# Loads in 1-KB runs, tokens kept by residue of four, and a list scheduler's engine orders, in a windowed attention followed by a gated MLP

## Chip, cores and metric

One core of one Trainium2 chip. The metric is device time in microseconds (us); a lower one is better. Every timed comparison below has runs of the kernel before on the same chip in the same rounds. The changed kernel was not run again beside the experiments, so where one is set against it, medians of different rounds and chips are compared; the kernel before had medians of 329.6 to 333.0 us in all of them. A run counts as slow when it is over 1.5% above the fastest of its kernel; ratios use fast runs alone. The output must match the reference; four experiments break that, and say so.

## The reference, cut

Eight batches, eight heads, 576 tokens, 64 columns per head. Heads 0 to 3 look back over 32 tokens ("plain"), heads 4 to 7 over 32 tokens at a distance of four ("dilated"). The result x (576 x 512 per batch) goes through a gated MLP with a shift by one token.

```python
mask_plain = (rel >= 0) & (rel < 32)
mask_dil   = (rel >= 0) & (rel < 128) & (rel % 4 == 0)      # heads 4..7
attn = softmax(where(mask, q @ k.T / 8, -1e9)) @ v          # [8, 8, 576, 64], f32
x  = attn.transpose(0, 2, 1, 3).reshape(8, 576, 512)
xk = mu_k * x + (1 - mu_k) * x_prev                         # "mixing", x_prev: x one token earlier
xr = mu_r * x + (1 - mu_r) * x_prev
k  = relu(xk @ w_k)                                         # 512 -> 1024
out = sigmoid(xr @ w_r) * (k * k @ w_v)                     # 1024 -> 512
```

## The kernel before

Tiles of q, k, v are loaded per batch; TensorE makes scores, ScalarE exponentials, VectorE masks and normalizes; the result is transposed into `xT` (columns on partitions). `interp` mixes neighbouring tokens, and the MLP runs on tiles of 512 tokens. Attention of batch p and MLP of tile p-1 are woven by hand-given costs. The parts that matter here:

```python
p_s = tc.tile_pool(name="p_s", bufs=1, space=PSUM)   # scores, 2 banks
p_o = tc.tile_pool(name="p_o", bufs=2, space=PSUM)   # attention outputs and transposes
p_k = tc.tile_pool(name="p_k", bufs=2, space=PSUM)   # x @ w_k
p_v = tc.tile_pool(name="p_v", bufs=2, space=PSUM)   # x @ w_r, k2 @ w_v

def load(b):
    for nm, src, lst in (("q", q, qn), ("k", k, kn)):           # plain heads: runs of 256 B, SP
        for h in range(4):
            nc.sync.dma_start(out=t[:, h], in_=src[b, h].rearrange("(c p) d -> p c d", p=96))
    # ... dilated q and k: "h (p r) d -> p h (r d)", runs of 1 KB, cast on the way (GpSimd queue)
    # ... plain v in six windows of 128 tokens, runs of 256 B (SP)
    for r in range(4):                                          # dilated v: runs of 256 B, cast on the way
        nc.gpsimd.dma_start(out=VD1[i][:, r, :, 0:64], in_=vr[0:112, r, 4:8])
    # ... casts of q (DVE), k and v (POOL)

def interp(t0, n):
    dx = wrk.tile([128, 4, n], FP16, name=f"dx{n}", bufs=1)
    nc.gpsimd.tensor_tensor(out=dx, in0=xo, in1=xT[:, :, 1 + t0:1 + t0 + n], op=ALU.subtract)
    for mu, dst in ((nmk, xk), (nmr, xr)):
        # per column chunk: tm = dx * mu (DVE); then dst = tm + xT (DVE)
        ...
```

The softmax here doesn't subtract the row's maximum and nothing guards it: scores larger than these inputs give would overflow.

## Time and profile before

| | kernel before |
|---|---|
| median of four runs (lowest, highest) | 331.25 us (328.71, 413.53) |
| profiled span | 332.9 us |
| first MLP matmul (pk, the product with w_k) | 48.0 us |
| mixing of batch 1 done | 104.6 us |
| six periods, batch 1's mixing to batch 7's | 186.0 us, 31.0 each |
| from the last batch's mixing to the end | 42.3 us |

"Mixing done" is the end of the addition that makes `xk` for the last tokens of a batch. The three lower rows make up the span: 104.6 + 186.0 + 42.3 = 332.9. "Period n" is the stretch that ends with batch n's mixing. The kernel before mixes each batch in two parts, 384 tokens and 192: by the first parts the account is 93.1 + 190.1 + 49.7. The lines that the start rests on (start, length, engine, line, what, count, idle time before):

```profile
48.03 3.70 PE L381 MATMUL pk<-xk,wk 128*128 128x384 f16 x12
...
67.81 2.72 PE L381 MATMUL pk<-xk,wk 128*128 128x384 f16 x8 [14.62 <-DMA VD<-in_v_dram]
```

and of VectorE, the second part of batch 1, on which the first pk that reads batch 1 (at 104.7 us) waits:

```profile
104.07 0.56 DVE L338 TENSOR_TENSOR xk<-tm,xT 128x768 f16<-128x768 f16 x1
```

So the MLP begins at 48.0 us, and 67.8, which the prediction takes for its first matmul, is where it goes on after a hole of 14.6 us. The queues of the profile's page (packets, MB, share of the 16 DMA engines' time):

```profile
q1 hardware_dynamic: 86496, 29.31, 41.4%
q0 software_dynamic: 35920, 10.23, 31.9%
```

In these kernels the transfers that SP issues are on the hardware queue, those that GpSimd issues, the only ones that cast on the way, on the software queue. 41.4% of 332.9 us is 138 us of full activity, 31.9% is 106: 244 us in all. Activity is the sum of the packets' own times over 16 engines; packets overlap, so a share can exceed 1.

### The profile page before, as it was taken

The page shows a single profiled execution, that of the slowest core. Times are in us where ns is not written, and L with a number is a line of the kernel's source. Part 1 is how long each engine was busy: PE and PEld are TensorE (multiplying, and loading weights), DVE is VectorE, ACT ScalarE, POOL GpSimd, SP SyncE. Part 2 cuts the span into 40 slices and gives each one's busy share as a digit, 9 for nine tenths or more (in the row PEclk, how much of TensorE's full clock was granted, in tenths as well). Part 3 has the DMA queues.
Part 4 walks back from the last instruction along what each step waited for, and adds up shares of the span by engine and source line. Part 5 has one row for each costly group of instructions (what it writes and reads, how often), then busy time and mean ns, then how long its engine had stood idle before and what let it go on. Part 6 is the DMA issues. An engine that isn't in the chain of part 4 may idle for free.

```text
span 332.9 us, 5643 instructions
## 1 busy us (share of the span) xinstructions
PE 242.7 (73%) x2048; PEld 123.8 (37%) x2048; DVE 204.9 (62%) x569; ACT 141.0 (42%) x221; POOL 125.1 (38%) x143
## 2 busy tenths in 40 slices
PE   0234563087857984999398867979997997999995
PEld 0223432044523541444144423434443443444441
DVE  1224770088685778597768788877867776743321
ACT  1023422065405830773074526644663764444421
POOL 7584574356536158234831363246003103100000
PEclk9999999569975997799877999997999999999998
DMA  9999999999996997749983784363100100111112
GB/s 146 189 174 177 185 124 130 181 185 194 222 148 132 221 182 103 153 82 151 232 175 63 114 167 107 47 117 50 63 33 24 41 33 32 65 63 63 65 63 95
DMA packets 122443, 39.89 MB, mean 120 GB/s; under 512 B 106032, under 2 KB 117808, under 8 KB 122416
## 3 DMA queue, kind: packets, MB, share of 16 engines
q1 hardware_dynamic: 86496, 29.31, 41.4%
q0 software_dynamic: 35920, 10.23, 31.9%
q8 instruction: 16, 0.26, 0.3%
q14 instruction: 11, 0.09, 0.1%
HBM read 36.18 MB, written 9.44 MB: 137 GB/s over the span
## 4 chain that ended last, share of the span: by engine, by line
PE 43%; DVE 16%; DMA 11%; POOL 8%; ACT 8%; issue 7%; SPq 6%; POOLq 0%; DVEq 0%; ACTq 0%
PE pk L381 16%; PE pv L405 12%; POOL dx L332 8%; DVE tm L336 8%; PE pr L396 7%; DMA qkA<-in_q_dram 4%; ACT xT L285 3%; DVE xk L338 3%; DMA stq<-in_q_dram 3%; SPq L80 2%; SPq L90 2%; DMA VD<-in_v_dram 2%; PE po L237 2%; PE ps L210 2%; DVE k L385 1%
## 5 line engine op out<-in xcount | busy, mean ns | idle before, releaser
L381 PE MATMUL pk<-xk,wk 128*128 128x512 f16 (+2 forms) x320 | 87.6, 398 | 33.9 <-DVE xk L338 19.2
L384 ACT ACTIVATE kr<-pk 128x512 f16<-128x512 f32 (+2 forms) x80 | 44.2, 557 | 93.5 <-PE pk L381 70.1
L405 PE MATMUL pv<-wv,k 128*128 128x512 f16 x288 | 73.4, 382 | 1.5 <-DVE k L385 0.9
L332 POOL TENSOR_TENSOR dx<-xT 128x768 f16<-128x768 f16 (+1 forms) x17 | 34.4, 2023 | 84.8 <-ACT xT L322 36.8
L381 PEld LDWEIGHTS <-wk 128*128 128x128 f16 x320 | 29.5, 105 | 61.4 <-issue 45.3
L396 PE MATMUL pr<-wr,xr 128*128 128x512 f16 x144 | 41.3, 398 | 3.5 <-DVE xr L338 3.5
L385 DVE TENSOR_TENSOR k<-kr 128x512 f16<-128x512 f16 (+2 forms) x80 | 33.3, 422 | 15.1 <-ACT kr L384 15.0
L93 POOL DMA_DIRECT2D VD<-in_v_dram x32 | 22.5, 705 | 53.1 <-PE po L273 30.1
L408 DVE SCALAR_TENSOR_TENSOR ot<-th,pv 128x512 f32<-128x512 f32 x36 | 24.6, 685 | 23.9 <-PE pv L405 19.7
L336 DVE TENSOR_SCALAR tm<-dx,nmk 128x192 f16<-128x192 f16 (+1 forms) x68 | 23.3, 407 | 25.5 <-POOL dx L332 25.5
L405 PEld LDWEIGHTS <-k 128*128 128x128 f16 x288 | 26.2, 98 | 28.8 <-issue 2.2
L197 DVE TENSOR_TENSOR xs<-po,rc 96x256 f16<-96x256 f32 (+2 forms) x88 | 35.7, 416 | 0.9
L398 ACT ACTIVATE th<-pr 128x512 f32<-128x512 f32 x36 | 22.3, 619 | 26.4 <-PE pr L396 26.3
L190 ACT ACTIVATE qt<-pt 128x576 f16<-128x576 f16 x32 | 21.4, 672 | 26.6 <-PE pt L186 26.0
L216 ACT ACTIVATE atp<-ps 128x768 f16<-128x768 f32 x24 | 19.5, 811 | 19.1 <-PE ps L210 18.9
L237 PE MATMUL po<-VP,atp 128*128 128x65 f16 x192 | 14.4, 201 | 17.3 <-ACT xT L285 9.1
L97 DVE CAST qn<-stq 96x1536 f16<-96x1536 f32 x8 | 7.6, 950 | 28.9 <-DMA stq<-in_q_dram 28.9
L95 POOL DMA_DIRECT2D VD<-in_v_dram x32 | 19.9, 630 | 6.5 <-DMA qkA<-in_k_dram 3.7
L195 DVE RECIPROCAL rc<-po 96x4 f32<-96x4 f32 (+2 forms) x88 | 14.7, 172 | 12.3 <-PE po L237 11.3
L285 ACT ACTIVATE xT<-txd 128x448 f16<-128x448 f16 x16 | 18.7, 1167 | 8.0 <-PE txd L282 7.8
L336 DVE TENSOR_SCALAR tm<-dx,nmr 128x192 f16<-128x192 f16 (+1 forms) x68 | 21.0, 353 | 0.0
L237 PEld LDWEIGHTS <-atp 128*128 128x128 f16 x192 | 11.1, 102 | 25.5 <-issue 12.1
(63 smaller groups left out, 295.6 us busy)
## 6 DMA issues: line engine op xcount, KB each, us to landing
out_dram<-ot SPq DMA_DIRECT2D x36, 256.0 KB, 2.1
stv<-in_v_dram SPq DMA_DIRECT2D x48, 128.0 KB, 4.3
stq<-in_q_dram SPq DMA_DIRECT2D x32, 144.0 KB, 4.9
stk<-in_k_dram SPq DMA_DIRECT2D x32, 144.0 KB, 6.1
VD<-in_v_dram POOLq DMA_DIRECT2D x32, 56.0 KB, 4.9
qkA<-in_q_dram POOLq DMA_DIRECT2D x8, 192.0 KB, 5.1
qkA<-in_k_dram POOLq DMA_DIRECT2D x8, 192.0 KB, 6.4
VD<-in_v_dram POOLq DMA_DIRECT2D x32, 32.0 KB, 5.0
```

The lines of the kernel that those rows point to most:

```text
L93: nc.gpsimd.dma_start(out=VD1[i][:, r, :, 0:64], in_=vr[0:112, r, 4:8])
L197: nc.vector.tensor_tensor(out=xs[:n], in0=po[:n, :, 0:64], in1=rc[:n].unsqueeze(2).to_broadcast([n, 4, 64]), op=ALU.mult)
L237: nc.tensor.matmul(out=po[:, 2 * hp + par], lhsT=at[:, par * 4 + wl * 2 + hp], rhs=VP[vi][:, w, 2 * hp + par, 0:65], start=True, stop=True)
L285: nc.scalar.activation(out=ov[:, :, 2 * rp:2 * rp + 2], in_=tx, func=AF.Copy)
L332: nc.gpsimd.tensor_tensor(out=dx, in0=xo, in1=xT[:, :, 1 + t0:1 + t0 + n], op=ALU.subtract)
L336: nc.vector.tensor_scalar(out=t[:, c], in0=dx[:, c], scalar1=mu[:, c:c + 1], scalar2=None, op0=ALU.mult)
L381: nc.tensor.matmul(out=pk[:, 0:n], lhsT=wk[:, c, f * 128:f * 128 + 128], rhs=xk[:, c, t0 % RING:t0 % RING + n], start=(c == 0), stop=(c == 3))
L384: nc.scalar.activation(out=kr[:, 0:n], in_=pk[:, 0:n], func=AF.Relu, scale=0.5 ** 0.5)
L385: nc.vector.tensor_tensor(out=K2[i][:, f, 0:n], in0=kr[:, 0:n], in1=kr[:, 0:n], op=ALU.mult)
L396: nc.tensor.matmul(out=pr, lhsT=xr[:, c, a % RING:a % RING + 128], rhs=wr[:, c], start=(c == 0), stop=(c == 3))
L405: nc.tensor.matmul(out=pv, lhsT=K2[i][:, f, s * 128:s * 128 + 128], rhs=wv[:, f], start=(f == 0), stop=(f == NF - 1))
L408: nc.vector.scalar_tensor_tensor(out=ot, in0=K2[i, s], scalar=1.0, in1=pv, op0=ALU.add, op1=ALU.mult)
```

## The change

Its intent is threefold. First, all q, k and dilated v come as four consecutive tokens of 64 columns, one run of 1 KB, so that fewer packets carry the same data. Second, tokens stay ordered by residue of four all the way through attention, mixing and MLP, which makes the dilated heads' outputs contiguous, and the shift by one token a move from one residue to the next. GpSimd then keeps only casts and cast loads; the subtraction moves to VectorE, the r half's scaling to ScalarE. Third, each engine's order comes from a list scheduler that runs while the kernel is built: every operation states an assumed duration, its dependences and the buffers it holds. The attention's two PSUM pools with three slots become one pool of two slots, and the MLP's two pools one pool of four banks, as many as before. The scheduler places every operation anew after each edit.

The diff, cut to its core (cuts marked by "..."):

```diff
-def merge(a, b):
-    ...
+class Plan:
+    def op(self, eng, dur, fn, dep=(), use=(), prio=0.0, lock=False, lat=None, xfer=None):
+        ...
+    def run(self, pe_slack=0.12):
+        ...
+            if o.xfer is not None:
+                t_dma = max(t_dma, t + o.dur + 0.6) + o.xfer
+                o.end = t_dma + 1.5
+        ...
-    p_s = ctx.enter_context(tc.tile_pool(name="p_s", bufs=1, space=PSUM))
-    ...                                                       # p_o, p_k, p_v with 2 each
+    pools = {"qk": 2, "st": 7, "v": 2, "kqd": 2, "qt": 2, "at": 3, "xs": 3, "rc": 4, "xT": 2, "dx": 1,
+             "ring": NR, "kr": 2, "K2": 2, "th": 3, "ot": 3, "cm": 4, "pa": 2}
+    CM = many(4, [128, 512], FP32, "CM", psp)                 # MLP
+    PA = many(2, [128, 2, 512], FP32, "PA", psp)              # all of attention
-            for h in range(4):
-                nc.sync.dma_start(out=t[:, h], in_=src[b, h].rearrange("(c p) d -> p c d", p=96))
+    def qk_src(i, b, h0, h1, a, e):
+        return qs[i][b, h0:h1].rearrange("h (p r) d -> p h (r d)", r=4)[a:e]
+    def load_qk_cast(b, prio, after=()):                      # batches 1 to 7, GpSimd queue
+                nc.gpsimd.dma_start(out=qk_dst(bq.idx, i, 0, 8, part), in_=qk_src(i, b, 0, 8, a, e))
-        for r in range(4):
-            nc.gpsimd.dma_start(out=VD1[i][:, r, :, 0:64], in_=vr[0:112, r, 4:8])
+                nc.sync.dma_start(out=ST[s.idx][0:np_].rearrange("p (h x) -> p h x", h=4),
+                                  in_=v[b, 4:8].rearrange("h (p r) d -> p h (r d)", r=4)[a:e])
-            nc.gpsimd.tensor_tensor(out=dx, in0=xo, in1=xT[:, :, 1 + t0:1 + t0 + n], op=ALU.subtract)
+            nc.vector.tensor_tensor(out=DX[0][:, c0:c1, 1:4], in0=t[:, :, 1:4, 2:], in1=t[:, :, 0:3, 2:], op=ALU.subtract)
+            nc.vector.tensor_tensor(out=DX[0][:, c0:c1, 0], in0=t[:, :, 0, 2:], in1=t[:, :, 3, 1:NP + 1], op=ALU.subtract)
+            nc.scalar.activation(out=XR[:, c, :, a:a + n], in_=DX[0][:, c, :, o:o + n], func=AF.Copy, scale=nmr[:, c:c + 1])
-            nc.sync.dma_start(out=outf[a:a + 128, :], in_=ot)
+            nc.sync.dma_start(out=out[b].rearrange("(p r) d -> r p d", r=4)[r, x:x + n], in_=OT[ot.idx][off:off + n])
+        load_qk_cast(b, -90 + 10 * b, after=[W["wk", 3]] if b == 1 else [W["wv", 3]])
+        load_v(b, ("POOL", "POOL", "POOL", "POOL"), -90 + 10 * b + 0.5)
```

## The prediction

> **What bounds the kernel now.** I read the page's engine totals first, then the 40 slices, then the chain that ended last in order of time, and then a table of windows cut at the chain's own turning points.
>
> ```profile
> PE 242.7 (73%) x2048; PEld 123.8 (37%) x2048; DVE 204.9 (62%) x569; ACT 141.0 (42%) x221; POOL 125.1 (38%) x143
> ...
> PE   0234563087857984999398867979997997999995
> ...
> PEclk9999999569975997799877999997999999999998
> DMA  9999999999996997749983784363100100111112
> ...
> DMA packets 122443, 39.89 MB, mean 120 GB/s; under 512 B 106032, under 2 KB 117808, under 8 KB 122416
> ```
>
> No engine is full over the whole span. A slice is 8.3 us: TensorE stays thin for eight slices while DMA is at nine tenths or more, and DMA goes quiet from slice 27 on. So there are three regimes: a start bound by loads, a middle, and an end where TensorE is full. The chain in order of time says which wait closes each:
>
> ```profile
> 45.74 14.75 DMA qkA<-in_q_dram
> 61.03 6.78 DMA VD<-in_v_dram
> 67.81 2.72 PE pk L381 x8
> ...
> 250.44 2.76 POOL dx L332
> 253.22 1.07 DVE tm L336 x5
> 254.37 0.96 DVE xk L338
> 255.38 1.02 PE pk L381 x4
> ```
>
> The first MLP matmul (pk) starts at 67.8 us, and 21.5 us ahead of it are two waits that the profile puts to loads of later batches' q and v. Neither is an operand of pk; they stand ahead of it by program order or by a shared queue. Later, each batch ends in a serial chain: the subtraction on POOL, then the mixing on DVE, then pk. It shows as the largest POOL wait in the list of waits (36.8 and 34.4 us) and as holes in TensorE. The windows, one per batch between two such chains, size it:
>
> ```profile
> 88.00:123.30 35.30, 26.94 (x230) 13.43 (x230) 25.05 (x65) 15.91 (x25) 16.22 (x17) 0.81 1.11 174
> ...
> 250.40:278.30 27.90, 24.79 (x242) 12.66 (x242) 20.74 (x64) 16.11 (x26) 4.23 (x3) 1.00 0.10 39
> 278.30:287.00 8.70, 7.08 (x56) 3.33 (x55) 6.42 (x19) 2.25 (x5) 2.73 (x1) 1.00 0.08 30
> 287.00:333.00 46.00, 41.78 (x192) 18.56 (x190) 16.76 (x37) 16.10 (x27) 1.47 (x1) 0.98 0.18 69
> ```
>
> Columns: window, length, busy PE, PEld, DVE, ACT, POOL, clock, DMA share, GB/s. A period falls from 35.3 us with DMA full and a clock of 0.81 to 27.9 us with DMA empty and a clock of 1.00. The last 46 us are matmuls back to back. Account: 68 to start, 219 for seven periods, 46 of tail.
>
> **What the Trainium skill says.** "DMA: Bandwidth & Descriptors", Specifications: a transfer needs at least 512 B for line rate. The trace agrees: 106,032 of 122,443 packets are below that, and the full slices move only 124 to 222 GB/s. "TensorE: Matmul & The Clock Gate", Back-to-back issue gap: an isolated warm 512-column matmul takes N/2.4 + 2.5 ns, about 216 ns. The tail of the chain has eight pv matmuls in 1.73 us, 216 ns each. The clock gate of the same page agrees in direction: the low clocks lie where PE has holes. "VectorE: DVE Perf Modes", Mode 2x_1P: two-tensor fp16 work gets two elements per cycle if packed and aligned; the 1536-element xk addition took 946 ns, 0.62 ns per element. "ScalarE: Activation LUTs", What ACT_TABLE_LOAD costs: 186 ns + 0.833 ns per element, so 0.61 us at 512; kr took 0.60. But xT<-txd with 448 took 1.167 us, not 0.56: its output skips four tokens, and that doubled it here.
>
> **The change part by part.**
>
> *Loads.* Removed: q and k of the plain heads in 256-B runs, 2 x 2304 x 8 = 36,864 packets, and the dilated v's 176 x 16 x 8 = 22,528. Added: all q and k as 2 x 1152 x 8 = 18,432 runs of 1 KB (the dilated half, 9,216, was there) and v as 5,632. So packets fall by about 45,000, to some 76,000. On the queue rows, the hardware queue spent 41.4% of 332.9 us x 16 on 86,496 packets, 25.5 ns each, and the software queue 31.9%, 47 ns each. Removed: 36,864 x 25.5/16 = 59 us and 22,528 x 47/16 = 66 us; a net 9,216 more 1-KB q/k runs and 5,632 of v give back some 27 + 12 us. DMA falls from 244 to about 160 us of full activity: some 20 us per batch, below a period, but not negligible.
>
> *The start.* Weights now come through SP and ACT casts, ahead of batch 1, and the MLP no longer waits for batch 1. Up to the end of w_k, 1.2 + 0.8 + 1.2 + 0.7 + 2.1 = 6 MB must land; at about 200 GB/s that is 30 us. Batch 0's attention can start near 8 us (first data after some 6, a 0.95-us cast), and its chain took 20 to 45 us before, also hindered by loads. I put the first pk at 33 us, 35 earlier.
>
> *Residue order.* Convolution taps become plain slices. POOL loses the subtractions (34.4 us), the k casts (12.3) and half the DMA issues (42.4 for dilated v): I expect 50 us. ACT's dilated outputs become contiguous: 16 at 0.56 in place of 1.167, and 8 at 0.746 go to DVE. The price: 64 transposes of 64 columns per batch in place of 24, in pairs on two column halves. Three transposes took 0.13 us in the timeline, 43 ns each; halves running together give 64 x 0.022 = 1.4 us, unpaired 2.2, against 1.0.
>
> *Sums for a batch, from durations above.* DVE: three plain blocks of mask 0.58, reciprocal 0.18, norm 0.68 (two windows at once), copy 0.35: 5.4; two dilated 2.9; the tail block 1.35; mixing 1.07 + 0.75 + 4 x 0.35 + 2 x 1.4 = 6.0. Total 15.6. With the MLP's 1.125 tiles x (4 x 0.68 + 4 x 0.685) = 6.1: 21.8. ACT: evictions 2.6, exps 4.9, dilated 1.1, the r half of mixing 2.7, and MLP 8.2: 19.5. PE: 1.125 x 80 matmuls x 0.2155 = 19.4, attention some 6: 25.4. PE is the bound of the steady state, DVE at 86% close behind. Over the kernel: DVE 184, ACT about 168 (more than now), PE 155 + 48 = 203 us of full-clock work.
>
> *Order.* The changed kernel's PE list, counted between the last transposes of successive attentions, has 1.7, 15.5, 15.5, 11.2, 19.0, 20.7, 17.2 and 18.1 us of MLP at 0.2155 each, and 36.2 us after the last. So tail 36 in place of 46, and a hole of about 4 us before it, since tiles 7 and 8 need batch 7's mixing and only eight pv matmuls stand between.
>
> *Sum.* First pk at 33. Batch 1's casts wait for w_k, so land at about 43; its attention needs about 20 us, ending near 65, with tile 0 done at 52 and PE half idle. Six periods hold 17.0 + 6.3 = 23.3 us of PE on average; at 90% density (the old last period reached about 81% by the same count: 17.2 + 5.5 of 27.9) 25.5 us each, 153. Hole 4, tail 36.2/0.98 = 37, output 2. 65 + 153 + 4 + 37 + 2 = 261; I take 258, since a denser PE should also keep the clock nearer 1.00 than the 0.81 to 0.90 of the old middle.
>
> **The rivals.**
>
> *PE stays dense at once.* If batch 1's loads land earlier and the periods reach 23.5 us, 60 + 141 + 4 + 37 + 2 = 244. For it: the old middle lost most to DMA and to POOL's chain, and both go. Against: the list was fixed with assumed durations, and engines follow it in order; one late load stalls all behind.
>
> *PSUM slots or DVE become the bound.* All attention passes through two slots (three separate buffers before). A batch makes 22 uses, and from the durations each holds some 1.0 to 1.8 us: 33 us, 17 per slot at the least. If every use also waits a queue's half microsecond or more three times, about 1 us on average, it is 28 per batch. Then 65 + 168 + 43 = 276. The 86% of DVE speaks for it.
>
> *Loads keep the bound.* SP carries v loads, transposes and outputs in one line; a late q/k cast would block a transpose, the outputs behind it, and through three output buffers the MLP. At 30 us per period: 288. Against: DMA was at 0.10 to 0.22 in the last periods and its work falls by a third.
>
> *Nothing gained.* TensorE's own work rises by some 7 us, ACT's by 27. For no gain the periods would need 37 us, worse than with today's full DMA. I give it 2%.
>
> **Range and chances.** Rivals at 244, 276 and 288 stand around 258. The first three span the range: 238 (the first with the start 5 us better) to 282 (between the second and third). Faster by over 2% means below 325.6: 0.97. Within 2%: 0.02. Slower: 0.01.
>
> **What would show it.** The first pk at 30 to 36 us shows the start; 42 or later breaks it. Packets near 76,000 and POOL near 50 us show the counts. DVE near 184 and ACT near 168 show the sums; much more means the stride or mode assumptions are wrong. Attentions' ends 25 to 26 us apart show the steady state; if 28 or more with PE waiting for DVE or ACT, the slots won; if PE waits for DMA, the loads did. The last batch's end some 40 us before the finish shows the tail. The prediction is wrong if the order's assumed durations are off enough to leave PE below about 80% density after 70 us.

## The result, and the profile after

The changed kernel took 300.21 us (median of four runs, 297.64 to 303.31), the kernel before 331.25. The ratio is 0.9106, with a 95% interval of 0.8999 to 0.9212. Ratios here are the mean time of one kernel's fast runs over the mean of the other's in the same rounds, so not quite the ratio of the medians quoted. So it is faster by 9%, not by the 22% that 258 us would have been, and outside the range of 238 to 282.

The page of the changed kernel, same rows as the prediction shows of before, with the two queues:

```profile
PE 234.5 (79%) x2336; PEld 124.9 (42%) x2336; DVE 180.3 (60%) x355; ACT 161.6 (54%) x254; POOL 52.3 (18%) x75
...
PE   1544679922659995699899949997999899599994
...
PEclk9999979975576999599999997999999799999999
DMA  8999999999999999994752792054003102200322
...
q1 hardware_dynamic: 59584, 33.24, 50.0%
q0 software_dynamic: 16576, 8.26, 22.9%
```

The engine sums came out as predicted. A slice is now 7.5 us: counted from 0, PE is at work from slice 1 on, but thins out again in slices 8 to 10 with a clock of 0.7 to 0.5, and DMA stays at 0.9 until slice 17. In the account: batch 1's mixing is done at 89.2 us in place of 104.6; the six periods then take 170.3 in place of 186.0, the end 38.8 in place of 42.3. The 34.6 us that the span lost are 15.4 + 15.7 + 3.5. (By the first parts of the old batches they are 3.9 + 19.8 + 10.9.)

Windows between the ends of mixing (columns as in the prediction: window, length, busy PE, PEld, DVE, ACT, POOL, clock, DMA share, GB/s):

```profile
70.50:89.20 18.70, 9.96 (x142) 6.78 (x143) 12.90 (x23) 7.33 (x12) 5.90 (x8) 0.59 1.14 232
89.20:124.20 35.00, 29.06 (x351) 16.41 (x351) 22.54 (x40) 20.67 (x34) 12.59 (x16) 0.84 1.34 208
...
148.40:179.60 31.20, 26.62 (x270) 13.41 (x270) 20.37 (x46) 18.31 (x34) 7.22 (x8) 1.00 0.72 145
...
207.30:233.10 25.80, 23.79 (x263) 12.89 (x263) 19.49 (x40) 16.88 (x29) 0.00 (x0) 1.00 0.16 48
```

Only the late windows, with DMA below 0.2, look like the predicted steady state (25.8 us against 25.5). The window of period 2 (35.0 us) carries a DMA share of 1.34, and the stretch before 89.2 a clock of 0.59.

The first pk started at 30.0 us, 18 us earlier than before, and batch 1 was mixed 15 us earlier, but 24 us later than the 65 predicted. The chain in order of time shows on what (start, length, what):

```profile
55.78 5.47 SPq L457
...
63.41 6.99 DMA KQD<-QB
...
72.16 3.49 DVE AT L579
...
80.72 3.35 PE CM L795 x8
...
87.80 1.37 DVE XK L706
```

L457 is the DMA transpose of batch 1's dilated q and k, issued by SP. Its own instruction took 5.47 us to issue, the last one's data came at 70.4, and PE waited 7.2 us for it. The eight pv matmuls of L795 then took 3.35 us in place of 1.73, at a granted clock of 0.50 (0.59 is the mean of the window). "TensorE: Matmul & The Clock Gate", section Why this matters for your kernels, of the Trainium skill asks for no idle gap of PE above some 3 us. The trace agrees only in part: the half rate is on record from 63.4 us, where the gap of 7.2 us begins and not after it, and until 83.9. In the 3.4 us before it PE was busy for 2.1, with no gap over 1.2 us, so the gap can have kept the clock low but did not start it. Why were the transposes late? SP's own timeline (start, busy, queue, line, what, count):

```profile
46.60 2.64 SPq L457 DMA_TRANSPOSE KQD<-QA  x1
49.34 4.06 SPq L372 DMA_DIRECT2D ST<-in_v_dram  x3
53.50 2.18 SPq L389 DMA_DIRECT2D ST<-in_v_dram  x1
55.78 5.47 SPq L457 DMA_TRANSPOSE KQD<-QA  x1
```

SP issues in one order, and from 30 to 75 us it issues with no pause over half a microsecond. Batch 1's casts had landed by 44.2 us, but from 44.9 us on loads of batch 2's v stand ahead of and between batch 1's four transposes, and while other transfers are under way some of its instructions take longer to issue: 5.47 us here against 1.21 for the third and fourth of the four, and 1.22 to 1.32 in e4 with nothing else under way. So three theories went to the chip. **Order:** the order on SP costs batch 1 its head start (v loads ahead of transposes), and less volume or a better order gives it back. **Slots:** two PSUM slots bound the periods. **Price:** the price of the transfers was wrong, bytes count and not packets. (The expectations have letters of their own: A is the order, B the slots, C the volume of the transfers.) GpSimd's casts beside VectorE's masks and the results on SP's line were two smaller suspects.

### The profile page after: what moved, and what is told of

Its sections match the earlier page's. It is cut to its first block, busy times and chain, and to the rows that moved or that the text cites. A ratio compares the mean times of both kernels' runs of the same rounds, so it can differ in the third digit from the quotient of the medians.

```text
span 298.3 us, 5959 instructions
## 1 busy us (share of the span) xinstructions
PE 234.5 (79%) x2336; PEld 124.9 (42%) x2336; DVE 180.3 (60%) x355; ACT 161.6 (54%) x254; POOL 52.3 (18%) x75
## 2 busy tenths in 40 slices
DMA packets 76187, 41.87 MB, mean 140 GB/s; under 512 B 45440, under 2 KB 69504, under 8 KB 76160
## 3 DMA queue, kind: packets, MB, share of 16 engines
q1 hardware_dynamic: 59584, 33.24, 50.0%
q0 software_dynamic: 16576, 8.26, 22.9%
## 4 chain that ended last, share of the span: by engine, by line
PE 63%; DVE 17%; DMA 11%; SPq 5%; ACT 2%; issue 1%; POOL 0%; DVEq 0%; ACTq 0%; POOLq 0%
PE CM L752 24%; PE CM L795 18%; PE CM L788 9%; DVE XK L706 3%; DMA ST<-in_moe_w_k_dram 3%; DVE XK L698 3%; PE PA L433 3%; DMA out_dram<-OT 3%; DMA KQD<-QB 2%; DMA ST<-in_k_dram 2%; SPq L457 2%; DVE OT L799 2%; DVE XS L493 2%; PE PA L540 2%; PE PA L589 2%
## 5 line engine op out<-in xcount | busy, mean ns | idle before, releaser
L752 PE MATMUL CM<-XK,wk 128*128 128x512 f16 x288 | 77.8, 414 | 18.2 <-DVE XK L706 18.1
L795 PE MATMUL CM<-wv,K 128*128 128x512 f16 x288 | 69.9, 387 | 0.0
L756 ACT ACTIVATE KR<-CM 128x512 f16<-128x512 f32 x72 | 42.9, 598 | 30.6 <-PE CM L752 30.1
L799 DVE SCALAR_TENSOR_TENSOR OT<-TH,CM 128x512 f32<-128x512 f32 x36 | 24.7, 687 | 39.6 <-PE CM L795 33.2
L765 DVE TENSOR_TENSOR K<-KR 128x1024 f16<-128x1024 f16 x36 | 27.7, 770 | 23.6 <-ACT KR L756 23.5
L795 PEld LDWEIGHTS <-K 128*128 128x128 f16 x288 | 26.7, 99 | 30.2 <-issue 1.7
L788 PE MATMUL CM<-wr,XR 128*128 128x512 f16 x144 | 36.4, 380 | 0.0
L791 ACT ACTIVATE TH<-CM 128x512 f32<-128x512 f32 x36 | 21.4, 596 | 24.6 <-PE CM L788 21.0
L493 DVE TENSOR_TENSOR XS<-PA,RC 96x512 f16<-96x512 f32 (+2 forms) x48 | 30.9, 644 | 1.7 <-DVE RC L489 0.2
L702 ACT ACTIVATE XR<-DX,nmr 128x576 f16<-128x576 f16 (+2 forms) x36 | 23.2, 714 | 2.4 <-DVE DX L695 2.4
L445 ACT ACTIVATE KT<-PA 128x768 f16<-128x768 f16 (+1 forms) x16 | 10.4, 652 | 15.8 <-PE PA L433 15.7
## 6 DMA issues: line engine op xcount, KB each, us to landing
ST<-in_moe_w_v_dram SPq DMA_DIRECT2D x4, 512.0 KB, 10.9
```

The lines of the kernel that those rows point to most:

```text
L493: nc.vector.tensor_tensor(out=XS[xs.idx][0:n, 0:g].rearrange("p w (h d) -> p w h d", h=4), in0=fin(po)[0:n, :, :, 0:64], in1=RC[rc.idx][0: ...
L702: nc.scalar.activation(out=XR[:, c, :, a:a + n], in_=DX[0][:, c, :, o:o + n], func=AF.Copy, scale=nmr[:, c:c + 1])
L752: nc.tensor.matmul(out=o, lhsT=wk[:, c, f * 128:f * 128 + 128], rhs=XK[:, c, :, a0:a0 + 128], start=(c == 0), stop=(c == 3))
L756: nc.scalar.activation(out=KR[kr.idx][:, g], in_=CM[pk.idx], func=AF.Relu, scale=0.5 ** 0.5)
L765: nc.vector.tensor_tensor(out=K2[k2.idx][:, 2 * f2:2 * f2 + 2], in0=KR[kr.idx], in1=KR[kr.idx], op=ALU.mult)
L788: nc.tensor.matmul(out=CM[pr.idx], lhsT=XR[:, c, r, a:a + 128], rhs=wr[:, c], start=(c == 0), stop=(c == 3))
```

## The experiments

All edits are to the changed kernel unless said otherwise. "Mixing starts" are the starts of a batch's XK addition in the profiled run; "done" is 1.4 us later. In the changed kernel they are at 87.8, 122.8, 147.0, 179.5, 205.8, 231.7 and 258.1 us for batches 1 to 7.

### e1: v loads behind the transposes

```diff
+                VLD.setdefault(b, []).append(d)          # in load_v, for every v load
+            for o in VLD.get(b + 1, []):                  # in attention, after pd
+                o.dep += list(KDR.values())
```

> Only change: the v loads of batch b+1 (for b of 1 and up) are made to follow the four dilated q/k transposes of batch b, so the sync queue no longer holds the v loads of two later batches ahead of batch 1's transposes. Theory A (batch 1's hole is the order on the sync queue plus the backlog in the rings): the transposes of batch 1 land 10 to 20 us earlier, the last one near 55 us where it was 70.5; the end of batch 1's mixing falls from 89.2 to 70-78 us and the whole by 8 to 15 us, to 285-292. Theory B (attention's PSUM slots or VectorE set the pace, the loads are hidden): the total stays within 3 us of 300. Theory C (the volume of the DMA work, not its order): the hole moves to batch 2 and the total falls by under 5 us.

Measured: 296.4 us, ratio 0.9044 [0.8934, 0.9153], which overlaps the changed kernel's own 0.9106 [0.8999, 0.9212]. Batch 1's mixing starts at 76.9, 11 us earlier; batches 2 and 3 at 107.6 and 145.2, so period 3 took 37.6 us. Batch 1's last transpose landed at 57.5 us in place of 70.4. The order on SP did cause batch 1's hole, but removing it moved the hole to batches 2 and 3 and gave no clear gain. In the profiled runs the lead of 11 us shrinks to 2 at batch 3, is 9 again at batch 4 and 8 at batch 7. "Order" is half right: the local cause is shown, its worth for the end is not.

### e2: the v loads of batches 2 to 7 left out (wrong)

```diff
-  d = sp_dma(..., ld, ...)
+  d = sp_dma(..., ld, ...) if b < 2 else None              # both kinds of v; the casts read old data
```

> Wrong on purpose: the v loads of batches 2 to 7 are dropped, the casts from the staging buffers stay (they read old contents), so some 7.1 MB and 23,000 packets leave the sync queue. Upper bound for what the v loads cost. Theory A or C (loads bind up to 130 us): DMA share falls to some 60%, the hole at 63-70 us closes, batches 1 and 2 end near 70 and 96 us, the stall of the output DMA near 170 us is gone, total 265-278 us. Theory B (PSUM slots, VectorE): total 295-300, periods unchanged.

Measured: 282.16 us, ratio 0.8625 [0.8548, 0.8702], 18 us below the changed kernel. Batch 1 at 73.6, the next at 102.1, 129.8 and 159.3: periods of 27.7 to 29.5 us, with no hole. The volume of the loads and their place on SP are worth some 18 us together; this run does not part them. The time lies between the two forecasts. Periods still ran at 24 to 29.5, so something else holds too.

### e3: the scheduler told that transfers take 1.3 times as long

```diff
-                t_dma = max(t_dma, t + o.dur + 0.6) + o.xfer
+                t_dma = max(t_dma, t + o.dur + 0.6) + 1.3 * o.xfer
```

> Only the scheduler's belief: every transfer counts 1.3 times as long, which is the measured 217 us of DMA activity over the 171 us that its own numbers sum to. No operation is added or taken away, only the orders differ. If a plan that is true to the transfers is enough, the holes are filled with other work and the total falls by 5 to 15 us. If the order of the sync queue (prefetches of v ahead of transposes, fixed by priorities) is the cause, the total stays within 4 us of 300, since that order is not changed by it.

Measured: 327.3 us, three of its four runs slow, so there is no ratio, and the one fast run, 321.34, is only a hint that this order was worse. Its profile (a slow run, and not read for time) shows what the new order held: one TensorE wait of 15.1 us for a v cast on GpSimd, which stood in line behind a load that waited for a transpose. A truer assumption alone did not make a better order here; the idea failed, and the size of its loss stays open.

### e4 and e13: the transfers by themselves (wrong)

Kernels that only move data, phase by phase, with a barrier between:

```diff
+  nc.sync.dma_start(out=t[:, h], in_=src[b, h].rearrange("(c p) d -> p c d", p=96))                      # q, k: runs of 256 B
+  nc.sync.dma_start(out=t, in_=src[b, 0:4].rearrange("h (p r) d -> p h (r d)", r=4)[a:e])                # same bytes, 1 KB
+  nc.sync.dma_start(out=..., in_=v[b, 0:4, k0:k0 + 128].transpose([1, 0, 2]))                            # v windows, 256 B
+  nc.sync.dma_start(out=outf[128 * i:128 * i + 128, :], in_=B[...])                                      # results, 2 KB
```

> Wrong on purpose, a measurement: transfers alone, in six phases parted by a VectorE memset: (1) q and k of the plain heads of four batches in 256-B runs, 4.7 MB, (2) the same bytes in 1-KB runs, (3) the same, cast on the software queue, (4) plain v windows of four batches, 256-B runs, (5) eight transposes (two batches' worth), (6) the results in 2-KB runs, 9.4 MB. My prediction priced a packet alike whatever its length: (1) 18,432 x 25.5/16 = 29 us, (2) 7.3 us, (3) 13.5 us. If bytes rule instead, (2) takes at least 0.6 of (1), some 15 to 22 us, and (3) as long or longer. Between the two, (2) is 10 to 14 us.

> Wrong on purpose, the measurement of the transfers again, with phases that do not overlap: (1) q and k of the plain heads of four batches, 4.7 MB in 256-B runs; (2) the same bytes in 1-KB runs; (3) 4.2 MB of weights in 4-KB and 2-KB runs; (4) as (2), cast on the software queue; (5) the dilated v of four batches, 2.9 MB in 256-B runs, cast, as before; (6) the same in 1-KB runs, no cast, as after. If bytes set the time at the first measurement's 205 to 213 GB/s: (1) 22-24 us, (2) 23-28, (6) 14-17. If packets do, (2) and (6) are a third of that. (3) should run at 300-380 GB/s, as the weights did in the changed kernel. (4) 18-24 us; (5) 11,264 packets x 47/16 = 33 us by the mean price of the software queue before, 15-20 us if bytes rule.

Windows inside the phases of e4 (window, length, DVE, POOL, clock, DMA share, GB/s): q and k in 1-KB runs, v windows in 256-B runs, results in 2-KB runs:

```profile
68.00:86.00 18.00, 0.00 (x0) 0.00 (x0) 1.00 1.12 211
118.00:134.00 16.00, 0.00 (x0) 0.00 (x0) 1.00 1.02 197
189.00:212.00 23.00, 0.00 (x0) 0.00 (x0) 1.00 1.03 382
```

and of e13, q and k in 256-B runs, weights in 4- and 2-KB runs, dilated v in 1-KB runs:

```profile
16.00:26.50 10.50, 10.30 (x1) 0.00 (x0) 1.00 1.31 213
134.00:146.00 12.00, 0.00 (x0) 0.00 (x0) 1.00 0.85 321
174.00:186.00 12.00, 0.00 (x0) 0.00 (x0) 1.00 1.05 219
```

On the hardware queue, the same q and k go at 213 GB/s in 256-B runs and at 211 in 1-KB runs: a quarter of the packets, no gain. "DMA: Bandwidth & Descriptors", section Why small descriptors are slow, gives 256-byte pieces an overhead of 27% on trn2; these windows show 213 against 211 and 197 against 219. Eight transposes took 12.5 us. The 1-KB form also puts half of its loads on 48 partitions where the 256-B form has 96 throughout, so what is shown is that this rearrangement gained nothing. The phases of the software queue overlapped their neighbours in part (a phase ran ahead of its barrier), but each trace has a stretch in which only that queue moves packets: 1-KB runs of q and k, cast, were written at 171 GB/s (e4, 18 to 27 us), 256-B runs of dilated v, cast, at 63 (e13, 64 to 76 us). There small runs are slower; but GpSimd was issuing for all 12 us of the second stretch and for 6 of the 9 us of the first, so its issues may be the limit and not the packets. e16 was made for this queue.

### e5: three attention slots in PSUM, two banks for the MLP

```diff
-  ... "cm": 4, "pa": 2}       +  ... "cm": 2, "pa": 3}
-  CM = many(4, ...)           +  CM = many(2, ...)
-  PA = many(2, ...)           +  PA = many(3, ...)
```

> PSUM split otherwise: three two-bank slots for attention in place of two, two single banks for the MLP in place of four. Theory B of the prediction's rivals (two slots hold attention back): the undisturbed periods late in the kernel (25.8 and 26.4 us, 207 to 259 us) fall to 23-24 us, total 285-293 unless the MLP's two banks cost it back. If loads and queue order made the loss: the first three periods stay as they are, and the total stays at 300 or rises (up to 320), because relu and square of a pk group now hold up the next group.

Measured: 286.46 us, ratio 0.8724 [0.8657, 0.8792], 14 us below the changed kernel. Batch 1 is unmoved (its mixing starts at 88.8), and the gain lies in the later windows:

```profile
90.20:125.00 34.80, 26.34 (x294) 13.92 (x294) 23.10 (x39) 19.99 (x33) 14.85 (x19) 0.90 1.30 197
...
148.20:167.20 19.00, 18.02 (x180) 8.80 (x181) 15.29 (x32) 16.20 (x31) 4.29 (x5) 1.00 1.10 201
...
192.40:213.70 21.30, 20.61 (x207) 10.87 (x206) 18.25 (x38) 13.03 (x22) 0.00 (x0) 1.00 0.19 46
```

PE is busy for 95 and 97% of the last two, against 85 and 92% in the changed kernel's windows of 31.2 and 25.8 us. PE's list of waits (line, releaser: us in total, times, longest) says on what it had waited; first the changed kernel:

```profile
PE CM L752 <- DVE XK L706: 18.1, 8, 4.6
```

then e5:

```profile
PE CM L752 <- DVE XK L706: 7.3, 3, 3.3
```

With a third slot attention runs further ahead, and its last product, the mixing, is ready when the MLP asks. By batch 7's mixing e5 leads by 21.6 us, 12.9 of them from period 4; 9.3 are paid back after it, where 48.1 us remain in place of 38.8. "Slots" is real. Because batch 1 does not move, it is another cause than that of "Order". No run parts the slot itself from the new orders that it allows.

### e6: v casts from GpSimd to ScalarE and VectorE

```diff
-        load_v(b, ("POOL", "POOL", "POOL", "POOL"), -90 + 10 * b + 0.5)
+        load_v(b, ("ACT", "ACT", "DVE", "DVE"), -90 + 10 * b + 0.5)
```

> Only change: the v casts of batches 1 to 7 leave GpSimd; the plain halves go to ScalarE, the dilated ones to VectorE. What it tests: (i) GpSimd's queue holds a v cast behind q/k loads of a later batch that wait for transposes, and (ii) VectorE's fast operations stretch while GpSimd casts (mask 3.49 us at 72 us, 2.46 us at 114.7 us against 0.6 and 0.4). ScalarE rises by some 12 us to 173, VectorE by 10 less the stretches (some 9 us) to about 181. If these mattered, the total falls by 4 to 10 us. If only the sync queue's order and the transfers count, it stays within 3 us of 300 and the hole at 63-70 us stays.

Measured: 291.68 us, ratio 0.8876 [0.8829, 0.8924]. The two lines below are the mask multiplication of the dilated heads (minimum/median/maximum ns), first in the changed kernel:

```profile
L579 DVE TENSOR_TENSOR AT<-AT,M x16: 611/624/3480, 28.2 to 247.9; 112x896 f16<-112x896 f16 x16
```

then in e6:

```profile
L579 DVE TENSOR_TENSOR AT<-AT,M x16: 608/624/627, 28.4 to 232.0; 112x896 f16<-112x896 f16 x16
```

Sixteen masks of one shape: 624 ns in the median of both, but the slowest took 3480 ns beside GpSimd's casts (the timeline has two casts, 2.02 us in all, and a third of 0.82 us begin within it: 2.84 us, and the mask took 2.86 longer), and 627 without them. "SBUF — State Buffer", section Who interferes with whom, of the Trainium skill says that a VectorE instruction with two inputs in SBUF contends with a GpSimd instruction that reads SBUF, and, for a port that is held, that the other is blocked for the whole instruction; these numbers agree. The slow mask at 72.2 us lay on the chain to batch 1, which now starts its mixing at 81.1, 6.7 us earlier. The mask's 2.86 us are less than half of that; as all orders changed too, the 8.5 us that e6 saves are not the contention's alone.

### e7 and e8: results on ScalarE's queue; and e1, e6 and e7 together

```diff
-  nc.sync.dma_start(out=out[b]..., in_=OT[ot.idx][off:off + n])
+  nc.scalar.dma_start(out=out[b]..., in_=OT[ot.idx][off:off + n])
-  sp_dma(128 * 0.084 / 16, lambda: out_dma(P0, r, ot), n=len(bs), dep=[f], use=[ot], prio=-1)
+  P.op("ACT", 0.08 * len(bs), lambda: out_dma(P0, r, ot), xfer=128 * 0.084 / 16, dep=[f], use=[ot], prio=-1)
```

> Only change: the results' transfers are issued by ScalarE's queue in place of the sync queue, so that they no longer stand behind transposes that wait for a buffer (10.6 and 9.4 us waits on the sync queue before 163 us, then an 8-us wait of an output and a 5-us wait of VectorE for its output buffer). Theory: the fourth period falls from 31.2 us to 26-28, total by 3 to 6 us, to 294-297; batch 1's hole is untouched (its end stays at 87-91 us). Against: if the issue costs ScalarE 0.4 us each time as it does the sync engine, 64 of them add 26 us to ScalarE and the gain is lost.

> Three changes together: v loads of a batch behind the transposes of the batch before, v casts moved to ScalarE and VectorE, results issued by ScalarE. If the holes up to 180 us are queue order (sync and GpSimd in-order queues), all go: batch 1 ends near 75 us, the next periods are 25-28 us, total 272-282 us. If the volume of transfers binds, with the same bytes as before, DMA stays at nine tenths until 130 us and the total is 288-296, as with the v loads alone.

Measured: e7 304.18 us, ratio 0.9281 [0.9202, 0.936], so no gain and rather a loss; period 4, which was to gain, did (29.5 us in place of 32.5 by the same count), but batches 1 to 3 came 2 to 6 us later, and an activation of ScalarE waited 11.1 us for a transpose. e8, the sum of three edits of which two had helped or done no harm, took 326.89 us, ratio 0.9927 [0.9825, 1.0028]: nearly all of the change's gain is gone, and both forecasts (272 to 282, 288 to 296) fail. Its list of waits points to the reason (engine, line, releaser: us in total, times, longest):

```profile
ACT TH L796 <- DMA KQD<-QB: 7.5, 1, 7.5
...
ACT KT L448 <- DMA ST<-in_v_dram: 6.0, 1, 6.0
```

ScalarE's activations waited for transfers that they do not read; other instructions waiting for those stood ahead of them in ScalarE's order. In both lines, and in e7's 11.1 us, these were the issues of results, which waited for a transpose (until 147.8 and 185.3 us here, 71.1 in e7; in the second line here a further one for a load of v); why they have to was not looked into. Gains of single edits do not add up where each puts a slow wait into an in-order engine. That the loss of e8 is made up of just these waits is argued from the list, not tested.

### e9: e5 and e2 together (wrong)

> Wrong on purpose: the third attention slot together with the dropped v loads of batches 2 to 7. If transfers and slots are the two causes and independent, their gains against the changed kernel add: 18 us (loads) and 14 us (slots) make 268; batch 1 ends near 74 us, the periods are 21-26 us. If one hides behind the other (the slots only matter while the loads press), the total stays at 274-280.

Measured: 268.17 us, ratio 0.8178 [0.8126, 0.8229]. e5 took off 14 and e2 18, together 32: the changed kernel's 300 less 32 is 268, so the two gains add, and neither hides behind the other, as was expected. The slices:

```profile
PE   1545549997794999999999999989999998999993
...
DMA  7999999999999749999234211630131033011232
```

From slice 13 on PE is full. Between batch 1's mixing and the last there are 139.1 us, 23.2 per period with PE busy for 137.4 of them: that is the predicted "dense" rival (23.5), reached only with a quarter of all read bytes gone.

### e10, e11, e12, e15, e17: combinations that give the right result

All have e5's slots. e10 adds e1; e11 adds e6; e12 lets batch 1's q and k loads wait for less; e15 puts all v casts on VectorE; e17 is e11 with one more score and one more normed buffer.

```diff
 e12
-        load_qk_cast(b, -90 + 10 * b, after=[W["wk", 3]] if b == 1 else [W["wv", 3]])
+        load_qk_cast(b, -90 + 10 * b, after=[W["wk", 0]] if b == 1 else [W["wv", 3]])
 e15
-        load_v(b, ("POOL", "POOL", "POOL", "POOL"), -90 + 10 * b + 0.5)
+        load_v(b, ("DVE", "DVE", "DVE", "DVE"), -90 + 10 * b + 0.5)
 e17
-  ... "at": 3, "xs": 3, ...   +  ... "at": 4, "xs": 4, ...
```

> The third attention slot together with the v loads moved behind the transposes of the batch before. Adding the two gains alone (14 and 4 us) gives 282; if batch 1's end falls to some 77 us, as with the moved loads alone, and the later periods keep the 19-25 us of the third slot, it can reach 274-280. If the moved loads only shift the hole to batches 2 and 3, it is 284-290, no better than the slot alone.

> The third attention slot together with the v casts on ScalarE and VectorE. Adding the gains alone (14 and 8.5 us) gives 277. If the casts' gain was from the same waits as the slots' (late attention steps), 283-287. Batch 1's end near 81 us, as with the casts alone.

> The third attention slot, and batch 1's q and k loads wait for the first quarter of w_k only, in place of the last. If batch 1's lateness is the time at which its loads are issued, its end falls from 88.8 to 80-85 us and the total to 278-283. If it is the backlog and the sync queue's order (transposes behind v loads), the end stays at 87-90 us and the total at 286, and the first pk may come 1 to 4 us later.

> The third attention slot, v casts of batches 1 to 7 all on VectorE (about 2.5 us a batch at fast rate), none on ScalarE or GpSimd. If what is left at batch 1 is in-order queues that wait for v and VectorE's operations stretched by GpSimd's casts, batch 1 ends at 80-84 us and the total is 278-283, like the version with both engines or a little better, as ScalarE waits for nothing. If VectorE is then the bound (197 us of work), 285-292.

> The best version so far (third attention slot, v casts off GpSimd) with four in place of three score buffers and four in place of three buffers of normed outputs. With three PSUM slots these may now be the next limit: then the periods fall by 1 us or so each and the total by 3 to 8 us, to 275-280. If not, it stays within 3 us of 283.

| run | us | ratio to before, 95% | mixing starts, batches 1, 2, 4, 7 |
|---|---|---|---|
| changed kernel | 300.21 | 0.9106 [0.8999, 0.9212] | 87.8, 122.8, 179.5, 258.1 |
| e5 slots | 286.46 | 0.8724 [0.8657, 0.8792] | 88.8, 123.6, 166.4, 236.5 |
| e10 + v late | 283.5 | 0.8627 [0.8572, 0.8683] | 79.1, 117.4, 169.5, 235.9 |
| e11 + casts | 282.79 | 0.8594 [0.8541, 0.8647] | 84.3, 109.6, 154.1, 219.6 |
| e12 + batch 1 early | 288.04 | 0.8777 [0.8712, 0.8843] | 77.7, 115.3, 164.2, 229.4 |
| e15, all v casts DVE | 284.07 | 0.8573 [0.8489, 0.8657] | 84.1, 112.6, 161.5, 234.8 |
| e17, e11 + buffers | 280.78 | 0.8547 [0.8403, 0.8691] | 82.7, 110.6, 155.1, 219.1 |

e12 is the most instructive of them. Its edit did not do what it was meant for: batch 1's q and k loads were issued at 22.4 us and landed by 44.0 (23.2 and 44.4 in e5). But the scheduler gave SP another order, with batch 1's transposes further ahead of batch 2's v, and the last landed at 63.5 us in place of 71.8: in effect e12 is another test of "Order". It brought batch 1 forward by 11 us against e5 and was still 7 us ahead at batch 7's mixing, yet it took no less time: what remains after that mixing grew from 48.1 to 55.8 us. TensorE's work is the same in both. The profiled runs say where the lead went. This is e12's window of period 2, to be held against the first line of e5's windows:

```profile
79.00:116.70 37.70, 32.05 (x423) 18.32 (x422) 25.31 (x53) 23.27 (x38) 9.87 (x12) 0.86 1.21 195
```

PE was busy for 32.1 us of it, in e5's for 26.3, with the clock at 0.86 and 0.90. Over the whole span PE was busy for 239.9 us in e12 and 232.2 in e5, for the same 2336 matmuls, with a granted clock of 0.929 to 0.94 against 0.944 to 0.95 in the timed runs. So PE idled 7 us less (46.7 in place of 53.8 us) and worked 8 us longer. Attention was served first and MLP work was left for the end; e12 met neither of its forecasts. Why the clock was lower was not tested. e11 and e17 show the same: batch 7 is mixed 17 us earlier than in e5, but 60 and 56 us remain after it, and the time falls by 4 and 6 us.

Taking the casts off GpSimd helps a little (e11's interval is just clear of e5's), and where they go made no difference that these runs show (e11 and e15 overlap). e17 is the fastest kernel with the right result, 15% below before and 6 to 7% below the changed kernel; its difference to e11 is within the intervals.

### e14: the kernel before, with only the subtraction moved to VectorE

```diff
-            nc.gpsimd.tensor_tensor(out=dx, in0=xo, in1=xT[:, :, 1 + t0:1 + t0 + n], op=ALU.subtract)
+            nc.vector.tensor_tensor(out=dx, in0=xo, in1=xT[:, :, 1 + t0:1 + t0 + n], op=ALU.subtract)
```

> The kernel before with one line changed: the subtraction of shifted tokens on VectorE in place of GpSimd. My reading of the kernel before says that each batch ends in a chain of GpSimd's subtraction (2.75 us), the mixing and pk. On VectorE it takes 1.0 us[...], and stands in VectorE's own line: 1 to 2 us less per batch and some 1 us for the second part, total 8 to 18 us less, 312-322. If the chain is covered by the static order of steps, the total stays within 4 us of 330.

Measured: 306.46 us, ratio 0.9229 [0.9132, 0.9326], more than expected. Its subtraction in the groups by form (count | busy, mean ns | idle before):

```profile
L332 DVE TENSOR_TENSOR dx<-xT 128x1536 f16<-128x1536 f16 x7 | 6.7, 962 | 3.9 <-ACT xT L285 3.9
```

against this one on GpSimd in the kernel before:

```profile
L332 POOL TENSOR_TENSOR dx<-xT 128x1536 f16<-128x1536 f16 x7 | 19.2, 2748 | 39.8 <-ACT xT L285 34.4 <-issue 5.4
```

The vector engine does in 0.96 us what took GpSimd 2.75, and it sits in the chain mixing - pk of each batch. One line of the old kernel brings 25 us (331 x 0.0771), against 30 us for the whole change (331 x 0.0894). In the account e14 has 99.0 + 163.5 + 42.2: its six periods are shorter than the changed kernel's 170.3, and only the start (89.2) and the end (38.8) are better there. TensorE's granted clock rose as well, from 0.926 to 0.947 in the fast runs before to 0.955 to 0.966; how much of the 25 us is the clock was not separated.

### e16: the q and k loads of the changed kernel in 256-B runs again

```diff
-  nc.gpsimd.dma_start(out=qk_dst(...), in_=qk_src(i, b, 0, 8, a, e))
+  [nc.gpsimd.dma_start(out=qk_dst(...)[:, :, 64 * r:64 * r + 64], in_=qk_src(i, b, 0, 8, a, e)[:, :, 64 * r:64 * r + 64]) for r in range(4)]
   # and the same for batch 0's uncast loads on SP
```

> One part of the change undone in place: each q and k load is issued as four, one for each token residue, in runs of 256 B, with the same bytes to the same buffers, queues and order of everything else. Packets rise by 3 x 18,432 = 55,000 to some 131,000; GpSimd issues 112 q/k loads in place of 28 (some 55 us more of its time, at 0.65 us each). If bytes set the time on both queues, DMA activity stays near 73% of the span and the total is 298-306. If packets do, as my prediction priced them (25.5 to 47 ns), the loads of each later batch take some 20 us of activity more and the total is 315-340.

Measured: 316.1 us (two of four runs slow), ratio of the fast ones 0.9653 [0.943, 0.9877], so slower than the changed kernel. Its queues, over a span of 310.4 us:

```profile
q1 hardware_dynamic: 66880, 33.25, 47.4%
q0 software_dynamic: 66304, 8.26, 44.3%
```

On the software queue the packets went from 16,576 to 66,304 with the same 8.26 MB, and the activity from 22.9% of 298.3 = 68 us to 44.3% of 310.4 = 138 us. There, activity grew with the packets: 69 us more for 49,728 more, 22 ns each over 16 engines. On the hardware queue 7,296 more packets left the activity at 147 us (149 before). GpSimd's busy time doubled too (52.3 to 109.5 us), as it issues four times as many loads, so the loss in time may come from either. That bytes alone set the price does not hold for the software queue, by packets or by issues; on the hardware queue nothing here contradicts it.

## Why the prediction was wrong, by its own steps

The sum was 65 + 153 + 4 + 37 + 2 = 261, taken as 258. The same terms as measured: batch 1 done at 89.2 (+24.2); six periods with the hole 170.3 for 157 (+13.3); end 38.8 for 39 (-0.2). Together 298.3, the profiled span; the remaining 5 us of the miss of 42 are the 3 us taken off by hand and the 1.9 us between span and time.

**Right.** Packets (76,187 for 76,000, though the step's own sum gives 77,900), GpSimd's busy time (52.3 for 50), VectorE's (180.3 for 184), ScalarE's (161.6 for 168), the first pk (30.0 us for 33; "35 earlier" was a misreading of the chain, since the first pk before was at 48.0 and not at 67.8: it came 18 earlier), the end (38.8 for 39), and the late periods (25.8 and 26.4 for 25.5). Also the direction, and that the loads, the slots and SP's line were the rivals to fear.

**"DMA falls from 244 to about 160 us of full activity."** The failed term of the loads. It was measured at 50.0% + 22.9% of 298.3 us, or 217 us. The step charged every packet of a queue the queue's mean time (25.5 and 47 ns), so that removing packets removed time. On the hardware queue the mean packet grew with its bytes: 29.31 MB in 138 us before, 33.24 MB in 149 us after, which is 212 and 223 GB/s over 16 engines, while the time per packet rose from 25.5 to 40 ns (149 us x 16 / 59,584). e4 and e13 show it in isolation: 213 GB/s in 256-B and 211 in 1-KB runs. The "59 us" for the plain q and k were therefore the price of their bytes, which the change still moves. The step also left out the weights: 5.2 MB that the change moves from the software queue to the hardware queue. On the software queue the forecast came out nearly right (106 to 68 us; 66 less and 27 more were forecast), but partly by luck: e16's price there is 22 ns a packet, not 47.

**"Its attention needs about 20 us, ending near 65."** The largest failed term, 24 us. The step took batch 1's casts to land at 43 and nothing to stand between them and the attention. The casts did land at 44.2. The trace showed SP's loads of batch 2's v ahead of the transposes, a wait of 7.2 us, a mask of 3.5 us and half the clock. e1 and, by its new order, e12 eased the first of these, e6 the mask, and batch 1 moved by 7 to 11 us. An earlier batch 1 is not worth as much at the end, though: e1 was ahead by 11 us there, by 2 at batch 3 and by 8 at batch 7, and its time differs from the changed kernel's by less than the intervals tell; e12 kept a lead and paid it back in a longer end. The early stretch is paced by loads, as in the rival "loads keep the bound": DMA stays at 0.9 until slice 17, and with the v loads gone (e2) 18 us go too.

**"Six periods ... at 90% density 25.5 us each."** Right where DMA is quiet, wrong in periods 2 and 4 (35.0 and 31.2). The step held the rival "PSUM slots" to be one of three ways to go, with its 276 as an alternative. e5 shows that it was at work, for 14 us. It was not VectorE, which the prediction gave as the argument for that rival: VectorE's busy time hardly changed (180.3 to 177.7 us).

**The range.** It was drawn as if one rival at a time could come true: 276 or 288. Two did. e9 shows that they add: 14 + 18 = 32 us less, 268. That their own extra terms, 18 and 30 us on 258, would have made 306, near the 300 measured, is luck: both terms lie in the periods, and most of the miss (24 of 42 us) lies before them, at batch 1.

**What stays open.** The 10 us between 268 and 258. In e9 batch 1 is still done only at 84.6, 20 us later than predicted, and the periods at 23.2 make good for most of it; casts on GpSimd and the low clock around 70 us are still in it, but no run took them away together with the v loads. How much of the 9% comes from the residue order and how much from the scheduler was not separated either. e14 shows that one line, in the old layout, has 25 of the 30 us; it does not show that the subtraction is what gained them in the new one.

## What to carry to other kernels

Price a transfer by its bytes and its queue from a run of it alone, not by the mean time of a packet: the mean moves with the size, and merging runs paid only on the queue that casts on the way. Put no transfer that nobody needs soon ahead of one that an engine waits for on the same in-order queue, and no slow wait into the order of an engine that has other work, but do not expect an earlier batch to be an earlier end: in e12 the work of TensorE only moved behind it. Check what an edit did to the orders before you name its cause: here a scheduler redid them with most edits. When rivals act on different stretches of the span, add their costs before drawing the range, and try the one-line change first: here it had most of the gain.

## What the Trainium skill lacked or had wrong

- "DMA: Bandwidth & Descriptors", Specifications (at least 512 B for line rate): on the hardware queue here, 1-KB runs were no nearer to line rate than 256-B ones (211 and 219 against 213 and 197 GB/s); 2-KB and 4-KB runs reached 321 (weights) and 382 (results), but on 128 partitions, where the 1-KB runs had 48 to 112; no run parts the two. On the software queue with a cast, four times the packets for the same bytes doubled the activity (68 to 138 us). The page gives one threshold for both.
- "DMA: Bandwidth & Descriptors", Why small descriptors are slow: the 27% for 256-byte pieces did not show (213 against 211 GB/s in e13 and e4).
- No page that I found gives the time that a transfer's instruction occupies the issuing queue when DMA is full: SP's transposes took 1.21 to 1.32 us when they went quickly and up to 5.47 us among other transfers.
- "SBUF — State Buffer", Who interferes with whom, was borne out: 3480 ns in place of 624 for a mask beside GpSimd's casts. The page gives no size of the loss in a kernel; here it was 2.9 us on the chain, and moving the casts, which changed orders too, took off 8.5 us of 300 (e6).
